# Low weight parts of three blocks by accumulating transfers, wider state products in two units, and a last block pair split by token halves

## The chip, the cores and the metric

The kernel runs on one core of one Trainium2 chip. The metric is the device time of one execution in microseconds. Of the kernel before, three runs took 699.57, 699.68 and 700.46 us; the median is 699.68 us. The profile is of one further execution.

## The reference

There are two steps. The first is a gated linear recurrence over 768 tokens, for 4 batches and 8 heads of 48 dimensions: a complex state of 48x48 per head is turned and damped by a complex factor per token and dimension, the product of key and value is added, and the query reads the real part.

```
mag = sqrt(a_re*a_re + a_im*a_im);  scale = minimum(mag, 0.999) / (mag + 1e-6)
for t in range(768):
    S_re, S_im = ar*S_re - ai*S_im + k[t] (x) v[t],  ar*S_im + ai*S_re
    y[t] = einsum('bhd,bhde->bhe', q[t], S_re)
```

The second is a feed-forward without a nonlinearity other than a product: `x = y` as 3072 tokens by 384, `out = ((x @ w_a) * (x @ w_b)) @ w_out`, with 1536 columns in the middle. All inputs and outputs are float32.

## The kernel before, in words

**Units.** The work is cut into 12 units: two pairs of batches by six chunks of 128 tokens. A unit holds 256 tokens (two batches, i = 0 and 1). Per unit there are four stages. *Preparation* (`prep`, VectorE with ScalarE's help): cumulated products of the complex factors within the chunk, by which queries and keys are multiplied (L308, L323) so that the recurrence becomes a masked product of queries and keys. *Stacking* (`stack`, L345): ten copies within on-chip memory, issued by SP, which lay the prepared queries and keys out by head. *Attention* (`attn`): scores (L378, then the mask on VectorE, L381), transposes of the keys (L389, L393), outputs (L418, cast at L422), the residual of the rounding (L428; in units 0 and 1 by a product with a negative identity, L430 and L433), and the state update (`state`, products at L441, added by VectorE at L448 or, in the first chunk, copied by ScalarE at L450). *Feed-forward*: twelve blocks f of 128 middle columns.

**Feed-forward in rounded parts.** TensorE multiplies in the rounded format float32r. So each operand is split into a high part, which is the value rounded, and a low part, the rest: x is xh+xl, the weights are hi+lo, h is hh+hl, and a product is made of three, high by high, high by low and low by high. `gemm1` makes the 18 products of a block (L485), ScalarE copies one half of the result (L493), VectorE multiplies by the other (L494), ScalarE rounds it (L495) and VectorE takes the rest (L496). `gemm2` multiplies by w_out: for each half of the tokens (tt) three products (L503) are added in an accumulator that runs over all twelve blocks. A list `pend` holds a block's hh and hl back, so that `gemm2` of a block follows two blocks behind `gemm1` (LAG = 2). Behind the last block of a unit `second` copies each half from its accumulator (L642) and stores it from ScalarE's queue (L643).

**Weights.** They arrive as 64-bit floats, seen as pairs of 32-bit words. `split_weights` makes, for each block f and each of its three parts m (w_a, w_b, w_out, 384 columns each), a float32 value t in a buffer named o_sb by three bit steps on VectorE (L133, L135, L137). ScalarE rounds t into hi (L141). TensorE forms t - hi in an accumulator by two products with the identity and the negative identity (L146, L147; the first is float32 and runs in two passes), and ScalarE rounds that into lo (L148). The buffer o_sb exists three times (O_BUFS = 3) and is also used for the output. Accumulators of the conversion come from the pool of `gemm1` for blocks 0 to 6 and from the attention's pool `pm`, which has two buffers, from block 7 on.

**Order.** Python generators interleave the stages. Six blocks are converted before the attention of unit 0; block 6+f is converted ahead of block f of unit 0's feed-forward (w = 0). In the same loop the preparation of unit 1 is drained: 3000 ns of its written-in costs per block, and the rest when f is 4 (P1_AT), where the stacking of unit 1 is emitted too; the pieces of unit 1's attention are handed out from f = 5 on. The framework then places the instructions on each engine's queue by priority: `tc.high_priority` lifts the steps of the attention and, by more, those of the feed-forward. Each engine executes its queue in order. In the trace unit 1's attention begins only behind nearly all of unit 0's feed-forward.

**The end.** Behind the last loop the pieces of `chk` are tested (up to L698), then `second` runs for the two blocks left in `pend` (L699, L700), and a branch on the test result would start a slow exact path (`token_by_token`), which is not taken with these inputs.

## Time and profile before

| | |
|---|---|
| three runs | 699.57, 699.68, 700.46 us |
| the profiled execution | 700.52 us, its span 698.8 us |
| TensorE, products / weight loads | 654.6 us (94%) / 610.4 us (87%) |
| VectorE | 550.4 us (79%) |
| ScalarE | 311.4 us (45%) |
| GpSimd | 5.6 us (1%), 11 instructions |
| chain that ended last | PE 64%, DVE 26%, DMA 4%, ACT 3% |
| mean granted TensorE clock | 0.972 |

The span is the time from the first to the last recorded event of the program; the rest of the execution's time lies around it. In the profile PE is TensorE (PEld its weight loads), DVE VectorE, ACT ScalarE, POOL GpSimd; SPq and ACTq are the issue of transfers by SP and ScalarE. L141 is line 141 of the kernel. In a timeline a row has the start in us, the duration in us (the sum where several instructions are merged, with their count behind x), the engine, the line, the operation, output<-inputs, and in brackets how long the engine had been idle and what released it. In the table of groups the two numbers after the bar are the busy time in us and the mean of one in ns. Matmuls are pipelined, so the duration of one is longer than the distance to the next.

### The profile page before, as it was taken

To read this page: it belongs to the slowest core of one execution; us is meant where nothing else is said; L and a number is where in the kernel's file an instruction comes from. 1 tells how busy PE (TensorE), PEld (TensorE's weight loads), DVE (VectorE), ACT (ScalarE), POOL (GpSimd) and SP (SyncE) were. 2 spreads that over 40 slices of the span, in tenths; PEclk is the share of its full clock that TensorE was granted. 3 is DMA by queue.
4 is the path that set the end of the run, shared out by engine and by line. 5 is a ranking of instruction groups with operands and counts; after the bars stand their busy time and mean duration, and the time that the engine had idled before them with its cause. 6 is when DMAs were issued, how large, how long until landed. Compare 5 with 4: busy or idle time off the path is not lost.

```text
span 698.8 us, 14287 instructions
## 1 busy us (share of the span) xinstructions
PE 654.6 (94%) x5842; PEld 610.4 (87%) x5842; DVE 550.4 (79%) x1259; ACT 311.4 (45%) x622; POOL 5.6 (1%) x11
## 2 busy tenths in 40 slices
PE   3547999999999999999999999999999999999996
PEld 1224788799899999999999999999999999999996
DVE  6998899998888989989899798999989863233221
ACT  6357656634535446255363564534542332231221
POOL 3000000000000000000000000000000000000000
PEclk9567999999999999999999999999999999999999
DMA  8963300611414205124151340511510500300000
GB/s 312 403 262 93 120 1 0 180 58 58 130 38 130 81 21 157 58 88 132 32 161 45 93 143 2 166 69 47 135 55 2 162 27 17 106 23 2 24 1 27
DMA packets 30231, 63.93 MB, mean 91 GB/s; under 512 B 3664, under 2 KB 7248, under 8 KB 30160
## 3 DMA queue, kind: packets, MB, share of 16 engines
q1 hardware_dynamic: 26704, 58.23, 26.6%
q10 hardware_dynamic: 3456, 4.72, 1.9%
q8 instruction: 48, 0.79, 0.4%
q14 instruction: 23, 0.19, 0.1%
HBM read 39.32 MB, written 4.72 MB: 63 GB/s over the span
## 4 chain that ended last, share of the span: by engine, by line
PE 64%; DVE 26%; DMA 4%; ACT 3%; issue 2%; SPq 1%; DVEq 0%; ACTq 0%
PE ab L485 31%; PE o L503 15%; PE xp L418 6%; PE pm L378 4%; PE pm L441 4%; DVE a_t L288 2%; DMA w<-in_dram 2%; DVE pr L226 2%; DVE qk L308 2%; DVE h_t L494 2%; PE pm L389 2%; DVE hl L496 2%; DMA stk<-qk 1%; DVE am L381 1%; DVE z L232 1%
## 5 line engine op out<-in xcount | busy, mean ns | idle before, releaser
L485 PE MATMUL ab<-xh,w 128*128 128x256 f32 x1728 | 338.7, 285 | 0.0
L485 PEld LDWEIGHTS ab<-xh,w 128*128 128x128 f32 x1728 | 276.6, 189 | 1.9 <-issue 1.4
L485 PE MATMUL ab<-xl,w 128*128 128x256 f32 x864 | 244.6, 283 | 0.0
L485 PEld LDWEIGHTS ab<-xl,w 128*128 128x128 f32 x864 | 162.9, 189 | 0.5 <-ACT xl L433 0.2
L503 PE MATMUL o<-w,hh 128*128 128x384 f32 x576 | 152.4, 345 | 0.0
L493 ACT COPY h_t<-ab 128x256 f32<-128x256 f32 x144 | 53.3, 370 | 184.5 <-PE ab L485 184.1
L494 DVE TENSOR_TENSOR h_t<-ab,h_t 128x256 f32<-128x256 f32 x144 | 60.6, 421 | 70.5 <-ACT h_t L493 69.8
L503 PEld LDWEIGHTS o<-w,hh 128*128 128x128 f32 x576 | 96.8, 188 | 3.7 <-issue 2.8
L503 PE MATMUL o<-w,hl 128*128 128x384 f32 x288 | 97.6, 340 | 0.0
L495 ACT CAST hh<-h_t 128x256 fp32r<-128x256 f32 x144 | 58.0, 403 | 72.6 <-DVE h_t L494 71.4
L496 DVE TENSOR_TENSOR hl<-h_t,hh 128x256 fp32r<-128x256 f32 x144 | 60.6, 421 | 15.6 <-ACT hh L495 15.5
L378 PE MATMUL pm<-stk 128*128 128x128 f32 x384 | 55.3, 282 | 2.6 <-DMA stk<-qk 1.8
L146 PE MATMUL ab<-o_sb,ident 128*128 128x384 f32 x42 | 29.3, 797 | 29.9 <-DVE o_sb L137 29.9
L378 PEld LDWEIGHTS pm<-stk 128*128 128x128 f32 x384 | 49.6, 193 | 7.6 <-issue 4.2
L503 PEld LDWEIGHTS o<-w,hl 128*128 128x128 f32 x288 | 54.0, 188 | 0.1
L226 DVE TENSOR_TENSOR pr<-z 128x384 f32<-128x384 f32 (+1 forms) x91 | 47.2, 525 | 4.3 <-ACT z L212 2.5
L288 DVE TENSOR_TENSOR a_t<-z,b_t 128x768 f32<-128x768 f32 x48 | 45.1, 953 | 0.0
L146 PEld LDWEIGHTS ab<-o_sb,ident 128*128 128x128 f32 x42 | 10.2, 288 | 39.5 <-DVE o_sb L137 29.2
L418 PE MATMUL xp<-am,v_t 128*32 128x128 f32 x768 | 42.5, 277 | 2.1 <-DVE am L381 1.8
L308 DVE TENSOR_TENSOR qk<-qk,z 128x1536 f32<-128x1536 f32 (+1 forms) x26 | 42.3, 1628 | 0.1
L381 DVE TENSOR_TENSOR am<-pm,mask 128x512 f32<-128x512 f32 x48 | 32.8, 686 | 6.7 <-PE pm L378 6.6
L441 PEld LDWEIGHTS pm<-v_t,kt 128*96 128x96 f32 x320 | 32.2, 164 | 1.8 <-issue 1.4
(106 smaller groups left out, 758.7 us busy)
## 6 DMA issues: line engine op xcount, KB each, us to landing
w<-in_dram SPq DMA_DIRECT2D x36, 384.0 KB, 8.1
qk<-in_dram SPq DMA_DIRECT2D x12, 768.0 KB, 4.8
stk<-qk SPq DMA_DIRECT2D x48, 192.0 KB, 3.4
a_t<-in_dram SPq DMA_DIRECT2D x11, 768.0 KB, 4.4
v_t<-in_dram SPq DMA_DIRECT2D x24, 256.0 KB, 2.7
stk<-qk SPq DMA_DIRECT2D x24, 192.8 KB, 3.4
out_dram<-o_sb ACTq DMA_DIRECT2D x24, 192.0 KB, 1.9
stk<-qk SPq DMA_DIRECT2D x16, 128.0 KB, 3.1
```

Source lines behind the costliest of these rows:

```text
L226: vec.tensor_tensor(out=pr[:, :, :, o:o + n], in0=view(zz, W + at_(i) + 2 * o, [[W, 2], [-W, 2], [2, n]]), in1=tok(slice(1, 3), i - 1, o, ...
L288: vec.tensor_tensor(out=pz[:, s].rearrange("p (j b e) -> p j b e", j=SUB // 2, e=2), in0=zb[:, 1 + s], in1=view(bb, (1 + k - s) * NB, [[0, ...
L308: vec.tensor_tensor(out=qk4[:, :, k, x0:x1], in0=qk4[:, :, 1, x0:x1], in1=z[:, k].rearrange("p (j t) -> p j t", j=NJ).unsqueeze(2).broadca ...
L378: pe.matmul(out=sp[:, h4], lhsT=stk[:, h, ks], rhs=stk[:, h, qs], start=True, stop=True)
L418: pe.matmul(out=xp[qd * 32:(qd + 1) * 32, ti], lhsT=l, rhs=rr, start=st, stop=sp_, tile_position=(0, qd * 32), skip_group_check=True)
L441: pe.matmul(out=kp[0:KS, h4 * D:(h4 + 1) * D], lhsT=kts[i, hg][:, h4, :], rhs=v_t[:, o:o + D], start=True, stop=True)
L485: pe.matmul(out=ab[:, m * TOK:(m + 1) * TOK], lhsT=r(w_ab(f, part, m * NJ + i)), rhs=r(xt[:, i, :]), start=n == 0, stop=n == 8)
L493: act.copy(out=h_t, in_=ab[:, 0:TOK])
L494: vec.tensor_tensor(out=h_t, in0=ab[:, TOK:2 * TOK], in1=h_t, op=ALU.mult)
L495: act.copy(out=r(hh), in_=h_t)
L496: vec.tensor_tensor(out=r(hl), in0=h_t, in1=hh, op=ALU.subtract)
L503: pe.matmul(out=os_[tt][:, 0:DM], lhsT=r(ht[:, ts]), rhs=r(w_t[f, 2][:, part, :]), start=(f == 0 and n == 0), stop=(f == NF - 1 and n == 2))
```

## The change

There are three edits.

**Low parts of blocks 9 to 11.** All weight parts are now kept negative: hi is the negated rounding of t. For blocks 0 to 8 TensorE forms t + hi with the identity (a rounded copy `rident` is made at the start), and lo is the negated result. For blocks 9 to 11 (DMA_FROM) a transfer issued by GpSimd adds hi onto t in its o_sb buffer, and ScalarE rounds the negated t into lo (`round_late`) after the next piece's transfer has been emitted; what is left is rounded one step after block 11. Two negated factors cancel in the product of w_a and w_b; the sign of w_out is undone where the output is copied.

```
-act.copy(out=r(hi), in_=t)
+act.mul(out=r(hi), in_=t, mul=-1.0)
+if f >= DMA_FROM:
+    nc.gpsimd.dma_start(out=t, in_=hi, accum_op=ALU.add)
+    late.append((lo, t))
+    if len(late) > 1:
+        round_late()
+    continue
...
-pe.matmul(out=lp[:, 0:n], lhsT=r(nident), rhs=r(hi), start=False, stop=True)
-act.copy(out=r(lo), in_=lp[:, 0:n])
+pe.matmul(out=lp[:, 0:n], lhsT=r(rident), rhs=r(hi), start=False, stop=True)
+act.mul(out=r(lo), in_=lp[:, 0:n], mul=-1.0)
...
+while late:
+    round_late()
+yield
```

**State products of units 0 and 1.** The product of a head's keys and values takes 96 columns of the value tile instead of the head's own 48 (n is 2*D there, D in the other units); the columns of the head are picked where the result is read.

```
+own = u >= OWN_FROM
+n = D if own else 2 * D
-o = (h // 2) * 128 + (h % 2) * 80
+o = (h // 2) * 128 + (h % 2) * (80 if own else 32)
-kv = view(kp[0:KS], 0, [[2 * D, 2], [D, 2], [1, D]])
+kv = view(kp[0:KS], 0, [[2 * n, 2], [D if own else 3 * D, 2], [1, D]])
```

**The last two blocks.** The six products of the first token half (blocks 10 and 11) come before the six of the second. The first half is copied by ScalarE and stored by SP; the second is copied half by ScalarE and half by VectorE, and stored in two transfers, from ScalarE's and from SP's queue.

```
-while pend:
-    second()
+for tt in range(2):
+    for w2, f2, hh, hl, os2 in pend:
+        gemm2(f2, hh, hl, os2, (tt,))
+    o_sb = moe.tile([128, DM], F32, name="o_sb", bufs=O_BUFS)
+    if tt == 0:
+        act.mul(out=o_sb, in_=os2[tt][:, 0:DM], mul=-1.0)
+        sync.dma_start(out=out_d[w2, tt], in_=o_sb)
+    else:
+        act.mul(out=o_sb[:, 0:DM // 2], in_=os2[tt][:, 0:DM // 2], mul=-1.0)
+        vec.tensor_scalar(out=o_sb[:, DM // 2:], in0=os2[tt][:, DM // 2:DM], scalar1=-1.0, scalar2=None, op0=ALU.mult)
+        act.dma_start(out=out_d[w2, tt, :, 0:DM // 2], in_=o_sb[:, 0:DM // 2])
+        sync.dma_start(out=out_d[w2, tt, :, DM // 2:], in_=o_sb[:, DM // 2:])
```

More of the change, by code (lines that the diff above doesn't have):

```diff
@@ L45 @@
 HB = 3
+OWN_FROM = 2
 O_BUFS = 3
 CONV_ON_AB = 7
+DMA_FROM = 9
 NCHK = NU * G + NU + 1
@@ L114, in tile_kernel @@
     act.mul(out=nident.bitcast(F32R), in_=ident, mul=-1.0)
+    rident = const.tile([128, 128], F32, name="rident")
+    act.copy(out=rident.bitcast(F32R), in_=ident)
     w_t = {}
@@ L125, in load_weights, with round_late @@
                            in_=w_d[f, :, c0:c0 + n].bitcast(U32))
+    late = []
+    def round_late():
+        lo, t = late.pop(0)
+        act.mul(out=r(lo), in_=t, mul=-1.0)
     def split_weights():
@@ L497, in gemm1, with gemm2 @@
         return hh, hl
-    def gemm2(f, hh, hl, os_):
-        for tt in range(2):
+    def gemm2(f, hh, hl, os_, tts=range(2)):
+        for tt in tts:
             ts = slice(tt * 128, (tt + 1) * 128)
@@ L597, in feed_forward @@
                     o_sb = p1.tile([128, DM], F32, name="o_sb")
-                    act.copy(out=o_sb, in_=os_[tt][:, 0:DM])
+                    act.mul(out=o_sb, in_=os_[tt][:, 0:DM], mul=-1.0)
                     sync.dma_start(out=out_v[bass.ds(c, 1), bp, tt].rearrange("o p m -> p (o m)"), in_=o_sb)
@@ L641, in second @@
                 with tc.high_priority(offset=MOE_FIRST):
-                    act.copy(out=o_sb, in_=os2[tt][:, 0:DM])
+                    act.mul(out=o_sb, in_=os2[tt][:, 0:DM], mul=-1.0)
                 act.dma_start(out=out_d[w2, tt], in_=o_sb)
@@ L698, in tile_kernel @@
     vec.tensor_scalar(out=bad, in0=tot[0:1, 0:1], scalar1=128.0 * NCHK, scalar2=None, op0=ALU.not_equal)
-    while pend:
-        second()
+    for tt in range(2):
[3 more added lines that the diff above has]
+        if tt == 0:
+            act.mul(out=o_sb, in_=os2[tt][:, 0:DM], mul=-1.0)
+            sync.dma_start(out=out_d[w2, tt], in_=o_sb)
[4 more added lines that the diff above has]
+            sync.dma_start(out=out_d[w2, tt, :, DM // 2:], in_=o_sb[:, DM // 2:])
     fast.close()
```

4 lines of the change are left out of this document (2 added, 2 removed).

## The prediction

> **What bounds the kernel now.** I read the busy times by stage first, then the chain of work that ended last, then the timelines around the three places that the change touches. The stages:
>
> ```profile
> core 0: us, PE busy (x) PEld busy (x) DVE busy (x) ACT busy (x) POOL busy (x), PEclk, DMA share, GB/s
> 78.00:90.00 12.00, 12.00 (x93) 10.84 (x93) 10.32 (x24) 10.88 (x23) 0.00 (x0) 1.00 0.16 46
> 90.00:128.00 38.00, 37.66 (x239) 33.17 (x238) 37.44 (x95) 20.48 (x47) 0.00 (x0) 1.00 0.07 22
> 128.00:150.00 22.00, 20.08 (x245) 17.24 (x245) 19.83 (x47) 12.77 (x22) 0.00 (x0) 1.00 0.48 139
> 180.00:500.00 320.00, 318.57 (x3092) 306.78 (x3091) 290.77 (x648) 154.19 (x295) 0.00 (x0) 1.00 0.29 87
> ```
>
> From 180 us TensorE is full (318.57 of 320) at full clock, and the change touches nothing there but the last two microseconds. So the end is set by the moment at which the feed-forward of unit 1 can begin (150 us in this trace), and by the tail. The stage in which the change works, 90 to 128 us, is full on two engines at once: TensorE 37.66 of 38, VectorE 37.44 of 38; ScalarE has 17.5 us free. The chain of work tells which of the two carries on into the next stage:
>
> ```profile
> 118.19 0.54 DVE o_sb L133 x2
> 118.72 0.47 DVE o_sb L135
> 119.53 0.47 DVE o_sb L137
> 119.99 0.87 DVE a_t L317
> 120.86 0.47 DVE o_sb L135
> 121.72 0.40 issue
> 122.12 0.55 DVE o_sb L137
> 122.67 0.87 DVE qk L323
> 123.87 1.67 DVE qk L308
> 125.87 1.11 DVE qk L308
> 126.98 0.48 issue
> 127.57 3.38 DMA stk<-qk
> ...
> 132.22 1.41 PE o L503 x8
> ```
>
> It is VectorE: the preparation of unit 1 (L317, L323, L308) ends at 127.5 us, the stacking copies leave at 127.57, and only with their landing can unit 1's attention begin. TensorE, though busy, is at that time finishing unit 0's products (L503), for which nothing waits but its own next work. In the chain the reader should see the weight conversion (o_sb) standing between steps of the preparation: 0.54+0.47+0.47 us before L317 and 0.47+0.55 us behind it.
>
> **Low parts of blocks 9 to 11: what leaves TensorE.** Nine pieces (three blocks by three parts) lose an identity product in two float32 passes and a rounded one:
>
> ```profile
> 82.95 0.65 PE pm L146 x2
> ```
>
> 0.65 us for the two passes, and for the third 1.41/8 = 0.18 us, as L503 has it in the chain above: 9 x 0.83 = 7.4 us of TensorE between 97 and 123 us, and two psum buffers less in demand. Counted as time at the end this is nothing by itself, because VectorE's steps are all kept: the three bit steps of a piece stay, and the two casts on ScalarE stay (the second now reads memory instead of psum; both forms are casts of 128x384):
>
> ```profile
> L141 ACT CAST w<-o_sb 128x384 fp32r<-128x384 f32 x36 | 18.1, 510 | 12.3 <-DVE o_sb L137 11.5 <-DMA w<-in_dram 0.6
> ```
>
> The sign of all weights costs nothing, a scaled copy in place of a copy; the extra rounded identity is one ScalarE step at the very start, before any weight has landed.
>
> **What is added.** Nine transfers within on-chip memory, each 192 KB, issued by GpSimd, whose queue the page shows empty after its first microseconds. The trace has no transfer of GpSimd and none that accumulates. The nearest are the stacking copies, on-chip to on-chip:
>
> ```profile
> stk<-qk SPq DMA_DIRECT2D x48, 192.0 KB, 3.4
> DMA to landing us min/median/max: 2.4/3.3/5.3
> ```
>
> I bound the landing by 2.4 and 5.3 us and take 3.4, the row of equal size; an accumulation can hardly land before a plain copy of the same size. No bandwidth is fought over: the DMA share in 90 to 128 us is 0.07. What the transfer changes is how long a piece keeps its o_sb buffer, of which there are three. Before, a buffer comes free when the identity product and the first cast have read it; now it must also wait for the landing and the rounding. The first five of the nine pieces run from here
>
> ```profile
> 97.06 0.35 DVE L133 TENSOR_SCALAR o_sb<-w 128x384 uint32<-128x384 uint32 x1
> ...
> 106.09 0.55 DVE L137 SCALAR_TENSOR_TENSOR o_sb<-w,o_sb 128x384 uint32<-128x384 uint32 x1
> ```
>
> to here: 9.6 us for five, 1.9 us apart, 5.7 us for one turn of three buffers. A turn now needs some 2.5 us of bit steps as they are interleaved, two casts of 0.51 us and 3.4 us: 6.9 us. So each of these pieces comes about (6.9-5.7)/3 = 0.4 us later, 2 us over the five, and VectorE takes steps of the preparation in the meantime, which stand beside them in its order. The whole nine take 25.6 us (97.06 to 122.67), 8.5 us a turn, so that the later ones are not held. Two microseconds later means that the last piece's two steps (0.47 and 0.55 us at 120.86 and 122.12) fall behind L323 and L308 and leave the path. This is the gain that I count: 1.0 us, between nothing (they stay where they are) and 2.5 us (all the conversion steps of the quoted chain leave it). The last rounding then comes near 130 us; unit 0's last products wait for it, and nothing waits for them before the attention of unit 1 is through.
>
> **What that stage gains behind 128 us.** The ten stacking copies are issued one behind the other:
>
> ```profile
> 127.57 7.06 SPq L345 DMA_DIRECT2D stk<-qk  x10
> ...
> 138.84 0.49 PE L378 MATMUL pm<-stk 128*128 128x128 f32 x2 [0.57 <-ACT kt L393]
> ```
>
> 0.71 us each, so the tenth lands at 127.57 + 9x0.71 + 3.4 = 137.3 us; the scores that use it start at 138.84, 1.5 us later, held by work that queues on TensorE (L503, 1.41 us in the chain) and by ScalarE. With 7.4 us taken off TensorE the products of blocks 9 and 10 are mostly done before 131 us. I take 0.8 us, between 0 and 1.5. Against that, VectorE's four steps for blocks 10 and 11 may come ahead of L308 rather than behind it; I count that at nothing, since they then leave the stretch behind, and take it into the upper bound.
>
> **96 columns.** Units 0 and 1 do their state products 96 wide:
>
> ```profile
> 144.21 0.64 PE pm L441 x8
> ...
> 145.63 0.81 PE pm L389 x8
> ```
>
> 48 columns take 80 ns an instruction, the transposes, which move 96 columns, 101 ns. So 21 ns more, 0.17 us for a group of eight. In unit 1 three of the four groups lie before the feed-forward can begin: +0.5 us. In unit 0 the cost lies beside full VectorE. Bounds: 0 (if loading the weights sets the 80 ns) and twice the 0.64 us, +1.9 us for the three. VectorE and ScalarE read the same 192 columns as before. The Trainium skill, "TensorE: Matmul & The Clock Gate", section "LDWEIGHTS (loading the stationary operand)", gives a load as its columns over 1.2 in ns, 80 ns for the 96 here, which is what the row has; by that rule the weight load sets the pace and the sum has 0 instead of 0.5 us.
>
> **The tail.**
>
> ```profile
> 691.16 0.42 DVE L496 TENSOR_TENSOR hl<-h_t,hh 128x256 fp32r<-128x256 f32 x1
> ...
> 692.92 0.34 PE L503 MATMUL o<-w,hl 128*128 128x384 f32 x1
> 693.27 0.34 ACTq L643 DMA_DIRECT2D out_dram<-o_sb  x1
> 693.70 0.48 ACT L642 COPY o_sb<-o 128x384 f32<-128x384 f32 x1 [0.47 <-PE o L503]
> 694.21 0.56 ACTq L643 DMA_DIRECT2D out_dram<-o_sb  x1
> L450 ACT COPY u<-pm 96x192 f32<-96x192 f32 x8 | 2.5, 314 | 1.4 <-PE pm L441 1.4
> ```
>
> The twelve last products are the same, in another order; block 11's low part is ready at 691.58 us, and the sixth product, the first to use it, would start near 691.7, so TensorE still ends at 693.26. Then, before, ScalarE is in the issue of the first store and begins the second copy at 693.70; the store leaves at 694.21. After, the first half's copy and store (now on SP) lie half a microsecond earlier, both engines begin at 693.28 with 192 columns each, 0.31 us by L450, and two stores leave near 693.62: 0.6 us earlier. The bytes are the same; what comes behind the landing follows unchanged. I take -0.6 us, between -0.3 (two stores each pay for themselves) and -0.7.
>
> **Sum.** -1.0 -0.8 +0.5 -0.6 = -1.9 us. The profiled execution took 700.52 us (span 698.8 and 1.7 around it), 0.84 us above the median of the runs, 699.68; taken off the median, 697.8 us. A measurement of this kernel tells apart about 0.2%, 1.4 us. What is late next: the preparation of unit 2, which takes over VectorE at 127.8 and gets the slipped steps; if its stacking comes later, TensorE has feed-forward of unit 1 to do.
>
> **Rivals.** *The transfer hides and frees nothing*: the order of VectorE stays as it is, the scores wait for ScalarE and not for TensorE. Then -0.6 and 0 to +0.5 remain: 699.3 us. For it: VectorE's 37.44 of 38 us, to which the change gives nothing back.
>
> *More conversion slips*: all 2.5 us of the chain, with 1.5 us behind it, and 0.5 and -0.6 as above: -4.1, 695.6 us. Against it: the ScalarE steps between L302 and L317 leave VectorE gaps that the conversion fills for nothing.
>
> *ScalarE stands before a landing*: its queue is in order, and the rounding of a piece waits for its transfer. Behind it are queued L303 and L304, on which L317 waits, and the h_t copies, on which VectorE waits. Where the landing comes later than the place that the rounding was given, everything behind is late by the difference. Four pieces fall between 114 and 123 us; at 5.3 instead of 3.4 us, 1.9 us each, 7.6 us; ScalarE's free time (17.5 of 38 us, 46%) hides that share of it, leaving +4.1 us on the stacking. With +0.5 and -0.6, 703.7 us; at half that lateness 701.6. It decides from about 0.75 us of lateness a piece (4x0.75x0.54 = 1.6 us).
>
> *VectorE stands before a buffer*: 8.5 us a turn less 2.5 and 1.0 leaves 5.0 us for issue and landing together. Beyond that VectorE itself waits, a third of the excess for each of nine pieces: at 6 us, 9x1.0/3 = +3.0 us; with the other terms 702.6 us. The Trainium skill, "SBUF — State Buffer", section "Who interferes with whom", says that descriptors of GpSimd's transfers are written through ports that VectorE's two-port instructions lock, and advises against hiding such a transfer under VectorE; no run here shows one, and VectorE is what is full here.
>
> **Chances.** Forecast 0.33 (own range 696.6 to 698.3), hidden 0.32, more slips 0.13, ScalarE before a landing 0.13, VectorE before a buffer 0.09. Faster by over 0.2%: 0.46; within: 0.32; slower: 0.22. The range: from 695.0, past the rival of more gain and its weaker tail, to 702.3, which takes half of the two slow ones.
>
> **What would show it.** Right: no L146 after 97 us; stacking of unit 1 near 126.5 us; an L137 of block 11 behind L308; the score that was at 138.84 within 1 us of the tenth landing; L441 groups of 0.8 us; last stores near 0.6 us after TensorE's end less than now. Wrong: ScalarE idle before the rounding with a DMA as releaser, or VectorE idle before L133 with ScalarE's rounding as releaser; stacking after 128 us; landings over 5 us. If the stacking is earlier and the feed-forward of unit 1 is not, the loss lies in TensorE's order between.

## The result: 8.7 us slower, and the profile after

| | before | after |
|---|---|---|
| median of the runs | 699.7 us | 708.36 us (707.54 to 709.52, 4 runs) |
| ratio, 95% interval | | 1.0121 [1.0108, 1.0133] |
| profiled execution, span | 700.52, 698.8 us | 707.54, 705.3 us |
| mean granted TensorE clock | 0.972 | 0.958 |
| unit 1: first stacking copy issued | 127.57 us | 126.04 us |
| unit 1: first product of the feed-forward | 149.38 us | 151.87 us |
| unit 2: first stacking copy issued | 172.39 us | 177.61 us |
| TensorE's last product ends | 693.26 us | 698.56 us |
| from there to the span's end | 5.5 us | 6.8 us |

A second measurement of the changed kernel (last experiment below) gave 1.0112 [1.0096, 1.0129]. Of the 7.0 us between the two profiled executions 5.3 are there when TensorE ends, 1.2 more come behind it, and 0.5 lie outside the span. The 1.2 us do not repeat in full: in the second trace of the changed kernel (e18) 6.0 us lie behind TensorE's end, and in seven traces below that have the tail of before it is 5.4 to 6.3 us.

First the stages of the kernel after, in the same windows as before (columns: length, busy time and count of each engine, TensorE's granted clock, share and rate of the transfers):

```profile
90.00:128.00 38.00, 33.82 (x233) 31.57 (x231) 35.11 (x87) 18.71 (x43) 4.73 (x6) 0.99 0.24 52
128.00:150.00 22.00, 19.10 (x217) 16.19 (x216) 17.65 (x36) 14.05 (x24) 3.10 (x4) 0.78 0.63 150
180.00:500.00 320.00, 317.63 (x3045) 304.66 (x3046) 286.76 (x634) 150.46 (x290) 0.00 (x0) 1.00 0.30 88
```

From 180 us on TensorE is almost as full as before (317.63 against 318.57 us). Between 90 and 150 us TensorE now idles 7.1 of 60 us (2.3 before), and in the second stretch its clock is 0.78 instead of 1.00, which takes another 0.22 x 19.1 = 4.2 us of work. That is 9.0 us lost, 1.6 more than the 7.4 us of identity products that went. Some of the 5.3 us lies earlier: the stacking of unit 0 is issued at 60.37 us (58.74 before), the clock of 50 to 70 and of 70 to 90 us is 0.60 and 0.91 (0.68 and 1.00), and busy time times clock up to 90 us is 43.3 us instead of 45.6. The signs alone (e4) do the same there and lose no time, since TensorE then fills 128 to 140 us (11.95 of 12 us, 10.33 before); in the whole change it waits in that stretch instead. The 1.6 and the 2.3 us make 3.9 of the 5.3; the rest is not assigned. A finer cut of the later stretch finds the place, before first, then after:

```profile
114.00:128.00 14.00, 13.90 (x92) 12.49 (x91) 13.87 (x25) 8.74 (x18) 0.00 (x0) 1.00 0.17 59
128.00:140.00 12.00, 10.33 (x95) 8.62 (x98) 11.06 (x23) 9.22 (x15) 0.00 (x0) 1.00 0.70 201
```

```profile
114.00:128.00 14.00, 9.82 (x62) 8.69 (x60) 13.31 (x25) 7.09 (x16) 2.03 (x3) 0.98 0.40 97
128.00:140.00 12.00, 9.22 (x56) 7.13 (x55) 8.80 (x17) 7.25 (x12) 3.10 (x4) 0.60 0.86 183
```

What it waited for stands in the chain of the kernel after (start, duration, what; steps of 0.04 us and less are left out):

```profile
118.55 0.83 POOL o_sb L153
119.38 8.27 issue
127.67 4.91 DMA o_sb<-w
132.60 0.53 ACT w L135
133.18 1.65 PE o L524 x4
134.83 0.85 PE pm L397 x4
135.72 0.80 PE pm L397 x2
```

Read it upwards. The scores of unit 1 (L397, L378 before) begin in earnest at 134.83 us. Ahead of them in TensorE's order stand four products of unit 0 (L524, L503 before), which wait for a low part; ScalarE rounds it (L135, `round_late`) only when the transfer has landed, 4.91 us after its issue at 127.67. This is the sixth of the nine pieces, block 10's part of w_out. The 8.27 us before its issue are a wait too: GpSimd waits for the cast L151, and that for the piece's last bit step, L147, which has slipped behind the preparation of unit 1 (L327, L308 before) to 126.27 us. The timeline has the idle time before each step:

```profile
126.27 0.55 DVE L147 SCALAR_TENSOR_TENSOR o_sb<-w,o_sb 128x384 uint32<-128x384 uint32 x1
126.85 0.53 ACT L151 ACTIVATE w<-o_sb 128x384 fp32r<-128x384 f32 x1 [2.06 <-DVE o_sb L147]
127.67 0.86 POOL L153 DMA_DIRECT2D o_sb<-w  x1 [8.29 <-ACT w L151]
...
132.60 0.52 ACT L135 ACTIVATE w<-o_sb 128x384 fp32r<-128x384 f32 x1 [2.81 <-DMA o_sb<-w]
133.18 0.69 PE L524 MATMUL o<-w,hh 128*128 128x384 f32 x1 [1.66 <-ACT w L135]
134.62 1.90 PE L397 MATMUL pm<-stk 128*128 128x128 f32 x6
```

Five rows of the table of waits of the kernel after, 90 to 160 us (who <- for whom: us, times, longest):

```profile
ACT w L135 <- DMA o_sb<-w: 8.2, 5, 2.8
DVE o_sb L143 <- ACT w L135: 3.2, 2, 2.2
PE ab L506 <- ACT w L135: 2.2, 2, 2.0
PE o L524 <- ACT w L151: 1.9, 1, 1.9
PE o L524 <- ACT w L135: 1.7, 1, 1.7
```

ScalarE stands before landings, VectorE before a buffer that a rounding frees, and TensorE before casts (L151, L141 before) and roundings that are late. The landing itself is 3.0 us in the median of the four transfers that run alone (98 to 118 us; the longest took 4.4). Of the five from 118 to 142 us, whose median is 4.9, the first and the last land in 3.2 and 3.0 us; the three issued while the stacking copies run, from 127.67 us on, take 4.9, 5.6 and 6.3. The stacking copies get slower too: their ten issues take 9.91 us (7.06 before), and those of 192.8 KB land in 3.7 us (3.2 before).

```profile
o_sb<-w POOLq DMA_DIRECT2D x4, 192.0 KB, 3.0
```

```profile
stk<-qk SPq DMA_DIRECT2D x6, 192.8 KB, 3.7
o_sb<-w POOLq DMA_DIRECT2D x5, 192.0 KB, 4.9
```

```profile
126.04 9.91 SPq L364 DMA_DIRECT2D stk<-qk  x10
```

The tail of the kernel after:

```profile
698.22 0.34 PE L524 MATMUL o<-w,hl 128*128 128x384 f32 x1
698.60 0.33 ACT L729 ACTIVATE o_sb<-o 128x192 f32<-128x192 f32 x1 [0.21 <-PE o L524]
698.96 0.34 ACTq L731 DMA_DIRECT2D out_dram<-o_sb  x1
698.96 0.36 DVE L730 TENSOR_SCALAR o_sb<-o 128x192 f32<-128x192 f32 x1 [2.06 <-ACT o_sb L729]
699.35 0.86 SPq L732 DMA_DIRECT2D out_dram<-o_sb  x1
```

VectorE's half copy begins when ScalarE's has ended, not beside it, and the span ends 5.1 us after the end of the last store's issue (705.3 - 700.21); in the kernel before it is 4.0 us (698.8 - 694.77).

### The profile page after: what moved, and what is told of

The parts are those of the page before. It is cut to its first block, busy times and chain, and to the rows that moved or that the text cites. A ratio compares the mean times of both kernels' runs of the same rounds, so it can differ in the third digit from the quotient of the medians.

```text
span 705.3 us, 14260 instructions
## 1 busy us (share of the span) xinstructions
PE 655.8 (93%) x5815; PEld 609.9 (86%) x5815; DVE 552.7 (78%) x1260; ACT 312.0 (44%) x623; POOL 13.4 (2%) x20
## 4 chain that ended last, share of the span: by engine, by line
PE 56%; DVE 30%; issue 5%; ACT 4%; DMA 3%; POOL 0%; SPq 0%; DVEq 0%; POOLq 0%; ACTq 0%
PE ab L506 26%; PE o L524 13%; PE xp L437 6%; PE pm L397 5%; PE pm L462 4%; DVE a_t L307 3%; DVE qk L327 3%; DVE pr L245 2%; DVE hl L517 2%; DVE h_t L515 2%; PE pm L408 2%; DVE z L312 2%; DVE z L251 1%; DMA stk<-qk 1%; DVE pb L280 1%
## 5 line engine op out<-in xcount | busy, mean ns | idle before, releaser
L524 PE MATMUL o<-w,hh 128*128 128x384 f32 x576 | 152.6, 346 | 3.7 <-ACT w L151 1.9
L524 PEld LDWEIGHTS o<-w,hh 128*128 128x128 f32 x576 | 97.1, 189 | 7.8 <-issue 3.0
L524 PE MATMUL o<-w,hl 128*128 128x384 f32 x288 | 97.8, 340 | 0.1
L397 PE MATMUL pm<-stk 128*128 128x128 f32 x384 | 59.1, 290 | 2.9 <-DMA stk<-qk 2.7
L397 PEld LDWEIGHTS pm<-stk 128*128 128x128 f32 x384 | 51.4, 198 | 9.2 <-issue 6.0
L524 PEld LDWEIGHTS o<-w,hl 128*128 128x128 f32 x288 | 54.4, 189 | 0.4 <-DVE hl L517 0.4
L437 PE MATMUL xp<-am,v_t 128*32 128x128 f32 x768 | 44.0, 281 | 2.9 <-DVE am L400 2.7
L327 DVE TENSOR_TENSOR qk<-qk,z 128x1536 f32<-128x1536 f32 (+1 forms) x26 | 42.4, 1629 | 0.1
L437 PE MATMUL xp<-stk,u 128*32 128x128 f32 x640 | 35.3, 274 | 0.0
## 6 DMA issues: line engine op xcount, KB each, us to landing
stk<-qk SPq DMA_DIRECT2D x48, 192.0 KB, 3.3
stk<-qk SPq DMA_DIRECT2D x24, 192.8 KB, 3.4
out_dram<-o_sb ACTq DMA_DIRECT2D x22, 192.0 KB, 1.9
```

Source lines behind the costliest of these rows:

```text
L327: vec.tensor_tensor(out=qk4[:, :, k, x0:x1], in0=qk4[:, :, 1, x0:x1], in1=z[:, k].rearrange("p (j t) -> p j t", j=NJ).unsqueeze(2).broadca ...
L397: pe.matmul(out=sp[:, h4], lhsT=stk[:, h, ks], rhs=stk[:, h, qs], start=True, stop=True)
L437: pe.matmul(out=xp[qd * 32:(qd + 1) * 32, ti], lhsT=l, rhs=rr, start=st, stop=sp_, tile_position=(0, qd * 32), skip_group_check=True)
L524: pe.matmul(out=os_[tt][:, 0:DM], lhsT=r(ht[:, ts]), rhs=r(w_t[f, 2][:, part, :]), start=(f == 0 and n == 0), stop=(f == NF - 1 and n == 2))
```

## The experiments

The first theory was that the landing of the transfers carries the loss; the rivals were the tail, the wider products and the signs, and then the ways in which a landing can act. Each letter (theory A, B, C, D) holds for the run whose expectation names it; A for ScalarE's queue, B for the buffers, C for the missing work and D for TensorE's queue run through the transfers' part. A ratio is to the kernel before on the same chip; 0.1% is 0.7 us.

| kernel | edit | median us | ratio [95%] |
|---|---|---|---|
| e1_tail | tail alone | 701.13 | 1.0012 [1.0001, 1.0024] |
| e2_cols | 96 columns alone | 698.07 | 0.9962 [0.9946, 0.9978] |
| e3_dma | signs and transfers | 705.76 | 1.0071 [1.0054, 1.0088] |
| e4_sign | signs alone | 700.52 | 1.0002 [0.9990, 1.0014] |
| e5_dma_cols | e3 and 96 columns | 706.75 | 1.0082 [1.0067, 1.0096] |
| e7_dma_pool | e3, GpSimd rounds | 710.31 | 1.0152 [1.0137, 1.0166] |
| e9_no_transfer | e3 without the transfers | 700.80 | 1.0010 [0.9999, 1.0022] |
| e8_cols_tail | e2, tail on ScalarE's queue | 698.86 | 0.9981 [0.9972, 0.9991] |
| e10_own_memory | e3, o_sb free at once | 704.22 | 1.0066 [1.0051, 1.0080] |
| e11_own_memory_deep | e10, rounding three back | 704.79 | 1.0065 [1.0053, 1.0077] |
| e12_early_blocks | e3 for blocks 6 to 8 | 715.71 | 1.0225 [1.0202, 1.0249] |
| e13_halves | e2, token halves | 697.88 | 0.9970 [0.9958, 0.9982] |
| e14_no_round | e10 without rounding | 702.16 | 1.0030 [1.0016, 1.0044] |
| e15_no_transfer_cols | e9 and 96 columns | 698.69 | 0.9979 [0.9964, 0.9993] |
| e16_conv5 | before, five blocks ahead | 700.96 | 1.0010 [1.0000, 1.0019] |
| e17_best | e13 and e16 | 699.75 | 1.0001 [0.9989, 1.0014] |
| e18_after_again | the whole change | 707.88 | 1.0112 [1.0096, 1.0129] |
| e19_after_halves | the change, tail of e13 | 707.89 | 1.0102 [1.0082, 1.0122] |

### The four parts alone

**The tail.** The loop of the diff over token halves in place of `second`, with plain copies.

> Only the last two blocks by token halves, weights unsigned, everything else as before. In the profile of the change the span's end lies 6.8 us behind TensorE's last product against 5.5 us before, VectorE's half copy begins only when ScalarE's has ended, and SP's last store is issued at 0.8 us behind that product. Theory 1 (the tail itself lost what it was to save): slower than before by 1.0 to 1.6 us. Theory 2 (the tail saves 0.6 us as predicted and the late end came from elsewhere): faster by 0.3 to 0.7 us.

**The 96 columns.** OWN_FROM = 2 and the four lines of `state`.

> Only the 96 columns in units 0 and 1. Theory 1 (the weight load or the 96 columns set the pace, no change of order): 0 to +0.7 us. Theory 2 (the wider products also change the order in which the engines work and carry a part of the 8.7 us): slower by 2 us or more, with the stacking of unit 1 later than 127.6 us or the feed-forward of unit 1 later than 150 us.

**The transfers** with the signs that they need.

```
+OWN_FROM = 0
 DMA_FROM = 9
```

> Only the low parts of blocks 9 to 11 by accumulating transfers, with the sign of all weights; 48 columns and the old end. Theory 1 (ScalarE stands before landings and VectorE before buffers; this part carries the loss): slower by 5 to 8 us, ScalarE idle for 6 us or more with a transfer onto o_sb as releaser, the feed-forward of unit 1 at 151 us or later. Theory 2 (the three parts lose together through the order of work, none alone): within 2 us of before.

**The signs.**

```
+DMA_FROM = NF
```

> Only the sign of all weights (scaled copies, the rounded positive identity), every low part by products on TensorE, 48 columns, the old end. Theory 1 (the sign costs nothing): within 0.7 us of before. Theory 2 (scaled copies or the extra identity at the start delay unit 0, whose stacking came 1.6 us later in the change): slower by 1.5 us or more, stacking of unit 0 at 60 us or later.

The signs cost nothing that can be measured, the tail 0.8 us (0.1 to 1.7 by its interval), the transfers 5.0, and the columns do not cost but gain 2.7 us, which neither theory had. The transfers alone leave TensorE's end at 698.38 us, where the whole change has 698.56: the columns' gain is missing in the whole. Where the columns gain shows in their windows:

```profile
114.00:128.00 14.00, 14.00 (x95) 12.86 (x94) 13.84 (x24) 7.49 (x17) 0.00 (x0) 1.00 0.39 111
128.00:140.00 12.00, 12.00 (x137) 10.50 (x135) 10.82 (x24) 9.01 (x15) 0.00 (x0) 1.00 0.47 138
```

TensorE has no gap: 26.00 us busy, 24.23 before. The stacking of unit 1 is issued at 123.23 us instead of 127.57, and unit 0's last products (the last row starts at 150.17 us, 133.84 before) lie between the steps of unit 1's attention and fill the waits there.

### Does the columns' gain add to the transfers?

```
-OWN_FROM = 0
+OWN_FROM = 2
 DMA_FROM = 9
```

> The changed kernel with the tail of before: negated weights, accumulating transfers and 96 columns. Alone, the transfers cost 5.0 us (TensorE's last product at 698.38 us of the trace) and the columns gained 2.7. Theory A, the landings set x: once ScalarE and VectorE stand before transfers between 114 and 136 us, the feed-forward of unit 1 begins when they let it, and the order that the columns change no longer matters; then this kernel is as slow as the transfers alone or a little slower, +5 to +7.5 us against before, and the tail adds only its own 0.8 to 1.5 us to the 8.7 of the whole change. Theory B, the two parts add: +2.3 us, about 702; then about 6 us of the whole change come from the tail, which the trace of the changed kernel does not show.

1.0082 against 1.0071 for the transfers alone: no gain of 2.7 us is left, theory A. Without a landing it is there (0.9979 against 1.0010):

```
-nc.gpsimd.dma_start(out=t, in_=hi, accum_op=ALU.add)
+OWN_FROM = 2
```

> The kernel without transfers (the nine low parts are rounded from the weights themselves, nothing is subtracted) with the 96 columns added; tail of before. Without transfers and with 48 columns it was 700.8, its trace 1.7 us better at TensorE's end than before. If it is the landing alone that takes the columns' gain away, the gain is here: 1 to 3 us below the 48-column one, 697.5 to 700. If the two exclude each other in any case, because both come from the same slip of block 11's steps behind L308, it is within 1 us of the 48-column one, 700 to 701.5.

So the landing takes it away, and the two do not exclude each other.

### Is it the landing, or the missing work?

```
-nc.gpsimd.dma_start(out=t, in_=hi, accum_op=ALU.add)
```

> The transfers alone, less the transfers: the nine low parts are rounded from the weights themselves, nothing is subtracted (this part of the computation is left out), so neither an issue nor a landing is waited for; the identity products stay out of TensorE. Theory A or B, the landing (by ScalarE's queue or by the buffers) carries the loss: this kernel is as fast as before or faster, 696 to 700. Theory C, it is not the landing but that TensorE lacks the 7.4 us of identity products that kept it busy while VectorE prepared unit 1, so that its granted clock falls to 0.5 between 126 and 138 us: then the loss stays, 702 to 706, with the clock of that stretch below 0.8.

The loss is gone (1.0010, the interval holds 1), with the identity products still out of TensorE. Theory C falls as a cause of the loss, though its sign is there: the clock of 128 to 140 us is 0.89, and TensorE idles.

```profile
114.00:128.00 14.00, 11.24 (x65) 10.06 (x64) 14.00 (x24) 7.26 (x16) 0.00 (x0) 0.85 0.37 107
128.00:140.00 12.00, 10.41 (x116) 9.07 (x114) 9.19 (x20) 8.32 (x14) 0.00 (x0) 0.89 0.54 159
```

In this order of work that is the most that leaving the 7.4 us out could bring: TensorE idles 4.3 us of these 26 and runs slower, so even a transfer that lands at once gains nothing that could be measured; nor does it beside the columns (0.9979 with no landing, 0.9962 with the identity products in place).

### Who stands before the landing?

**GpSimd rounds** in place of ScalarE:

```
-act.mul(out=r(lo), in_=t, mul=-1.0)
+nc.gpsimd.tensor_scalar(out=r(lo), in0=t, scalar1=-1.0, scalar2=None, op0=ALU.mult)
```

> The transfers alone (negated weights, 48 columns, tail of before), with the rounding of a landed piece done by GpSimd, which has nothing else to do, in place of ScalarE. No ScalarE instruction then waits for a landing of a piece. Theory A, ScalarE's queue: its copies for the preparation and the score path no longer stand behind a landing, ScalarE's waits with a transfer of the pieces as releaser (11.1 us between 90 and 160) are gone, and most of the 5.0 us comes back: within 2 us of before, 698 to 702. Theory B, the buffers: VectorE's bit steps wait for a buffer that is held through issue, landing and rounding, whoever rounds; GpSimd's rounding is slower than ScalarE's, so VectorE's waits for a buffer grow and the loss stays or rises, 704 to 708.

Twice the loss. ScalarE no longer waits for landings, and it did not help, as theory B said. But B's reason carries little of it: VectorE's wait for a buffer is 1.7 us (0.2 in e3). TensorE waits 6.5 us for roundings (5.8 in e3), and ScalarE's copies of the transposed keys, in unit 1's attention, wait 9.0 us for TensorE (3.0 in e3):

```profile
ACT kt L412 <- PE pm L408: 9.0, 2, 7.8
PE ab L506 <- POOL w L135: 6.5, 2, 3.9
DVE o_sb L143 <- POOL w L135: 1.7, 1, 1.7
```

```profile
110.22 2.68 POOL L135 TENSOR_SCALAR w<-o_sb 128x384 fp32r<-128x384 f32 x1 [2.23 <-DMA o_sb<-w]
136.47 1.16 POOL L135 TENSOR_SCALAR w<-o_sb 128x384 fp32r<-128x384 f32 x1 [2.89 <-DMA o_sb<-w]
```

A rounding takes GpSimd 1.16 to 2.68 us (0.52 on ScalarE), and the low parts come later still. That gave theory D: what counts is when TensorE gets the low part, since its queue holds the readers ahead of unit 1's attention.

**The buffer.** The piece is copied to its place, the transfer adds there, and the rounding is done in place, one piece back and three pieces back:

```
-nc.gpsimd.dma_start(out=t, in_=hi, accum_op=ALU.add)
+act.copy(out=r(lo), in_=t)
+nc.gpsimd.dma_start(out=r(lo), in_=r(hi), accum_op=ALU.add)
-if len(late) > 1:          (e11: > 3)
```

> The transfers alone (48 columns, tail of before), but each piece is first copied by ScalarE into the place of its low part (nine more steps of 0.51 us), the transfer accumulates there, and the o_sb buffer is free once ScalarE has read it; the rounding still stands one piece behind in ScalarE's order. The copy rounds, so that the low parts of these blocks come out as zero: the subtraction is left out as arithmetic, not as work. The trace of the kernel without the transfers ended TensorE at 691.51 us, with them at 698.38. Theory B, the held buffers: VectorE's bit steps no longer wait for a landing and most of the loss goes, 699 to 702. Theory A or D, ScalarE's queue or TensorE's own queue before weights that come late: the landing is as late as before for both, 704 to 707.

> As the kernel with the transfer into the low part's own place, but the rounding stands three pieces behind instead of one, so that ScalarE meets it when its transfer has long landed. Low parts come out as zero here too. Theory A, ScalarE's queue: its waits with a transfer of the pieces as releaser fall below 1 us, and with the buffers free as well the time is near that of the kernel without transfers, 699 to 702, where the other of this pair stays at 704 or more. Theory D, TensorE's queue: unit 0's last products stand in TensorE's order before the scores of unit 1 and wait for the last low parts, which now come even later; the loss stays or grows, 704 to 708, with TensorE's waits for L135 as large as before (5.8 us between 90 and 160).

Neither moves the time beyond the intervals, so the buffers (B) do not carry the loss of e3, where VectorE waits 0.2 us for one. Both have nine copies more on ScalarE, which could hide a small gain. The 3.2 us of the whole change come with the columns (3.4 in e5) and were not tried by themselves. The three-back form does not do what it was made for: ScalarE still waits 8.7 us with a transfer as releaser, among them 2.5 us at 123.88 and 2.2 at 133.21, because the last pieces' bit steps come so late (126.7 to 129.7 us) that nothing is left to put between transfer and rounding. So it told A and D not apart.

**Nothing rounds behind the landing**; TensorE waits for it itself:

```
 nc.gpsimd.dma_start(out=r(lo), in_=r(hi), accum_op=ALU.add)
-late.append(lo)
-if len(late) > 1:
-    round_late()
```

> As the kernel with the transfer into the low part's own place (48 columns, tail of before), but nothing rounds behind the landing: the transfer's result is used as it lies, so no ScalarE step waits for a landing, and TensorE's products wait for it themselves. The nine roundings are left out as work. Theory A, ScalarE's queue before landings: the loss goes, 698 to 701. Theory D, the landing comes too late for TensorE, whose in-order queue holds the products of blocks 9 to 11 ahead of unit 1's scores: it stays, 703 to 706, and TensorE now waits with the transfers of the pieces as releaser for over 3 us between 110 and 140.

1.0030, between the two theories. Against 1.0066 with the rounding it is 0.36% or 2.5 us better, and the intervals do not meet: the nine roundings in ScalarE's queue, their waits with their work, carry about half of the loss. It is not the work of these steps: e3, with nine roundings where this kernel has nine copies, runs as many ScalarE steps and has 1.0071, and those intervals do not meet either. Against no transfer (1.0010) 1.4 us are left, with intervals that do meet, and these rows of the kernel without rounding say where:

```profile
PE ab L504 <- DMA w<-w: 2.2, 2, 1.9
PE pm L395 <- DMA stk<-qk: 1.5, 1, 1.5
```

TensorE waits for the landing of low parts (2.2 us, over 3 expected) and for stacking copies that share the transfers' time. So it is shown that a rounding which must wait for its landing costs about half of the loss. Whether it costs through ScalarE's later steps (A) or through low parts that reach TensorE later (D) is not separated: this kernel takes both away, and e7, which took only ScalarE's waits away, lost more.

**Earlier blocks.**

```
-if f >= DMA_FROM:
+if 6 <= f < 9:
```

> The transfers alone (48 columns, tail of before), but for blocks 6 to 8 instead of 9 to 11; the last three blocks keep the identity products. Everything is computed. Theory A and B, a landing holds ScalarE's queue and the buffers wherever it stands: VectorE is as full at 80 to 105 us as later, so the loss is of the same size, 703 to 707. Theory D, the place: the last blocks' low parts are what unit 0's last products wait for, directly ahead of unit 1's scores in TensorE's order; blocks 6 to 8 have other products to cover them, so the loss goes, 698 to 701, with TensorE's waits for L135 below 1 us.

Theory D named the last blocks as the bad place; the early ones are three times as bad, 715.71 us, and more than A and B expected too. There (60 to 105 us) the transfers meet the stacking copies of unit 0, for which TensorE waits with nothing else to do:

```profile
PE pm L398 <- DMA stk<-qk: 9.3, 4, 6.4
ACT w L136 <- DMA o_sb<-w: 9.2, 6, 1.8
```

```profile
o_sb<-w POOLq DMA_DIRECT2D x9, 192.0 KB, 4.9
stk<-qk SPq DMA_DIRECT2D x6, 192.0 KB, 4.8
```

Before, the six stacking copies of 192.0 KB in that stretch landed in 3.1 us. So there is a third path, which neither ScalarE's nor TensorE's queue explains: the two kinds of transfer are both slower when they run side by side, and the scores wait for one of them. The first six of the nine transfers, beside stacking copies and input loads, land in 4.8 to 5.8 us, the last three in 2.9 to 3.2. The changed kernel has this path too: in the trace of e18 the chain of work runs through the slowed stacking copies, the last of which lands at 138.09 us. What it costs there was not tried by itself.

### Why do the columns gain?

In their trace block 11's bit steps slip behind L308, the slip that the prediction had expected of the transfers. Five blocks ahead instead of six make that slip alone:

```
-CONV_FIRST = 6
+CONV_FIRST = 5
```

> The kernel before with one number changed: five blocks of weights instead of six are put into the order ahead of unit 0's attention, so that each later block, block 11 too, stands one block further back. Everything is computed. Theory A, the columns gained because the bit steps of block 11 slipped behind the preparation of unit 1: then this gains as much without any 96 columns, 696.5 to 698.5, with stacking of unit 1 at 122.5 to 125 in the trace (127.57 before). Theory B, the columns' gain has another source: within 0.2% of before, 698.5 to 701.3.

> 96 columns, token halves with whole copies stored by ScalarE, and five instead of six blocks ahead. Without the last it was 697.88. If the columns' gain is the slip of block 11, the slip is there already and a further one is late for TensorE's products of block 11: the same or a little slower, 697.5 to 700. If the two are separate, 695.5 to 697.

The stacking is 3.8 us earlier (123.75 us) and the time is not: 1.0010 [1.0000, 1.0019]. Theory A is not borne out. The windows of e16:

```profile
114.00:128.00 14.00, 13.54 (x90) 12.27 (x90) 13.95 (x26) 7.33 (x17) 0.00 (x0) 1.00 0.35 104
128.00:140.00 12.00, 11.03 (x113) 8.19 (x111) 11.41 (x23) 9.43 (x16) 0.00 (x0) 1.00 0.52 146
```

TensorE is busy 24.57 of 26 us (26.00 with the columns, 24.23 before): block 11 is converted so late that unit 0's last products wait with it, until 153.52 us. In this stretch an earlier stacking is worth only as much as TensorE has unit 0's products ready to put beside unit 1's attention. That the columns reach that mix is seen; why wider products move the order so is not settled. Added to the columns, the same number takes their gain away (1.0001).

But five blocks ahead is not the slip alone. It also leaves TensorE less to do before the scores of unit 0: in 50 to 70 us e16 is busy 14.75 us at a clock of 0.50, the kernel before 15.14 us at 0.68, some 2.9 us of work less. e17 has the same there (14.58 us at 0.50), while its 114 to 140 us are as full as with the columns alone (26.00 of 26 us). So in these traces the columns' gain goes in the early stretch, and what the slip alone is worth stays open.

### The tail

Three stores from ScalarE's queue, the half copies in two buffers (e8); whole halves by ScalarE (e13); the latter in the whole change (e19) beside the change itself (e18):

```
 if tt == 0: act.copy(o_sb); act.dma_start(o_sb)
 else:       act.copy(o_a, first half); vec.tensor_copy(o_b, second half)
             act.dma_start(o_a); act.dma_start(o_b)          (e8)
 for tt in range(2): gemm2(..., (tt,)); act.copy(o_sb); act.dma_start(o_sb)   (e13, e19)
```

> 96 columns alone, with a third form of the tail: token halves, the second half copied by ScalarE and VectorE into two separate buffers, and all three stores issued by ScalarE. Columns alone gave 698.07, 2.7 us under before. Theory A: the token-half tail lost 0.8 us because VectorE's half copy waited for ScalarE's (they write one buffer) and because the store on SP's queue put SP's branch at the end of the program behind it; then this one is 0.3 to 0.8 us faster than columns alone, 697.3 to 697.8, and the span ends under 5.5 us after TensorE. Theory B: it is the two last stores themselves that cost: then it is slower than columns alone by 0.3 to 0.8 us, 698.4 to 698.9.

> 96 columns alone, with the last two blocks by token halves, each half copied whole by ScalarE and stored from ScalarE's queue (no store from SP, no copy by VectorE). Columns alone: 698.07, TensorE's end to span's end 5.85 us in the trace. Theory A, the order by token halves is right and the split copies and SP's store were what cost: the first half's copy and store lie under TensorE's last six products, the second copy begins when they end, 0.4 us sooner; 0.3 to 0.5 us faster than columns alone, 697.6 to 697.8. Theory B, the order brings nothing, as what comes behind the last landing sets the end: within 0.2 us of columns alone.

> The changed kernel itself once more, as the measure for the run beside it. Transfers with columns gave +5.7 us, the tail alone +0.8. If the parts add, this is +6.5, 706 to 707.5 where before is 700; if the tail costs more inside the change, +8 to +9, 708 to 709.5.

> The changed kernel with the last token halves copied whole by ScalarE and stored from ScalarE's queue: no store from SP, no copy by VectorE; transfers and columns as in the change. With the columns alone this tail was as fast as the tail of before (0.9970 against 0.9962). Theory A, SP's store and the serialized half copies are all that the tail costs: 0.8 to 1.5 us under the run beside it, and the span ends under 6 us after TensorE's last product (6.8 in the changed kernel). Theory B, the difference lies between chips: then it is within 0.5 us of the run beside it.

The copies stay one behind the other in separate buffers (VectorE's row of e8, and the last store 0.98 us behind the one before it), so one buffer was not the reason; both read one accumulator.

```profile
691.14 0.88 ACTq L715 DMA_DIRECT2D out_dram<-o_sb  x1
691.14 0.36 DVE L714 COPY o_sb<-o 128x192 f32<-128x192 f32 x1 [2.29 <-ACT o_sb L713]
692.12 0.39 ACTq L716 DMA_DIRECT2D out_dram<-o_sb  x1
```

With whole halves the second copy still waits for the first store's issue, as in the kernel before:

```profile
690.41 0.34 ACTq L708 DMA_DIRECT2D out_dram<-o_sb  x1
690.85 0.48 ACT L707 COPY o_sb<-o 128x384 f32<-128x384 f32 x1 [0.47 <-PE o L506]
691.36 0.92 ACTq L708 DMA_DIRECT2D out_dram<-o_sb  x1
```

It is as fast as the columns with the old tail (0.9970 and 0.9962), not faster, as theory B of e13 had it. What SP's store costs is in the spans: from the end of the last store's issue to the span's end it is 5.0, 5.1 and 4.9 us where SP issues it (e1, the change, e18), and 4.0, 4.5, 4.0, 3.9 and 4.3 where ScalarE does (before, e2, e8, e13, e19). Some 0.9 us, about what the tail alone costs. This does not settle it: from the start of that issue the two groups overlap (5.2 to 6.0 and 4.4 to 5.3 us), and e8, without a store from SP, stands 0.19% above e2, near what its theory B (two last stores cost) had, though those intervals meet. Inside the change the two tails can't be told apart (1.0112 and 1.0102), e19 ends 6.1 us behind TensorE and not under 6, and e5 and e1 together give 0.94% where the whole gives 1.12 and 1.21%. The intervals of e5 and e1 added reach 1.20%, so the parts may add; up to 2 us more for the whole stay open.

## Why the prediction was wrong

Forecast 697.8 us, its range to 702.3; 708.36 came. The signs of both slow rivals, which were given 703.7 and 702.6, are in the trace.

- **What bounds the kernel: half right.** TensorE is full from 180 us on, and the stage before sets the end. But the forecast took the stacking of unit 1 as the time that carries over. It came 1.5 us earlier (126.04, forecast near 126.5), and the feed-forward of unit 1 2.5 us later. The forecast's own last line had named this case: the loss lies in TensorE's order between.
- **The step that failed** is the reading of TensorE at 127 us, "finishing unit 0's products (L503), for which nothing waits but its own next work". With it the wait of these products for a late low part was put at nothing. The forecast thought only of the last low part, and of that one it was right: one of block 11's products runs at 147.82 us and five from 156.24 on, behind nearly all of unit 1's attention. But the sixth part is late as well. At 133.18 us four products of block 10 stand in TensorE's queue ahead of the scores, behind 1.66 us of idle time, and the scores behind them (e18 has the same at 133.50). An engine's own order is a wait, also for work that needs nothing of what stands ahead. In all TensorE waits 5.8 us for casts and roundings between 90 and 160 us, and its clock falls. That the landings carry the transfers' loss is shown (1.0071 with, 1.0010 without); how it divides between TensorE's order, ScalarE's queue and the slowed stacking copies is read from waits and stays open. The last rounding was forecast near 130 us and began at 141.22.
- **Landing 3.4 us, no bandwidth fought over: wrong where it mattered.** 3.0 us in the median of the four alone, but 4.9, 5.6 and 6.3 for the three beside stacking copies, two of them above the upper bound of 5.3; landings over 5 us were also among the forecast's signs of being wrong. The forecast had looked at the share of 90 to 128 us (0.07), but the last transfers slip to 127 to 141 us, and the share of 128 to 150 us was 0.48 before, in a row that it had quoted.
- **Slips behind L323 and L308: right, but no gain is seen.** They did slip, and further than forecast: L147 of the last four pieces comes at 126.27 us and later, behind the second L327, which was L308. This took the transfers of these pieces to the time of the stacking copies. e16 has the slip without transfers and gains no time, but it loses work at 50 to 70 us as well, so whether the slip in itself is worth the 1.0 us is open.
- **0.8 us behind 128 us: wrong.** The scores were to be held less by TensorE, as its queue would be emptier. The queue was held instead.
- **7.4 us off TensorE counted as nothing: right**, and e9 bears it out: 1.0010 without landing.
- **96 columns, +0.5 us: wrong.** By themselves they gain 2.7 us, and in the change this gain is gone. A group of eight takes 0.85 us at 150.35 in the kernel after (0.81 forecast, 0.64 for 48 columns), so the price of an instruction was right; what the forecast left out is that the order of work changes. The Trainium skill, "TensorE: Matmul & The Clock Gate", section "LDWEIGHTS (loading the stationary operand)", would have 80 ns for each by the load; the row has 106.

```profile
150.35 0.85 PE pm L462 x8
```

- **The tail, -0.6 us: wrong, +0.8 alone.** The last store's issue starts 0.79 us after TensorE's end instead of 0.95, so 0.16 us of the 0.6 came: the half copies ran one behind the other. "What comes behind the landing follows unchanged" did not hold: from the end of the last issue to the span's end it is some 0.9 us more with SP's store. Which part of the tail costs the 0.8 us is open, as said.
- **Rivals.** ScalarE before a landing (8.2 us of waits, forecast 7.6 with 4.1 on the path) and VectorE before a buffer (3.2 us) are both in the table of waits. Of the first it is shown that roundings which wait cost time (e14); the second was not separated. The rule of the Trainium skill, "SBUF — State Buffer", section "Who interferes with whom", that VectorE's two-port instructions keep GpSimd from writing the descriptors of its transfers, does not account for the slow ones here, as far as the trace shows: the issues take 0.84 to 1.19 us, the transfer at 118.54 landed in 3.2 us with VectorE busy all the time, and the one at 127.67 in 4.9 us with VectorE busy 3.30 us of it. Which of VectorE's instructions were two-port ones the trace does not tell.

The first rival's +4.0 (703.7) is near the transfers' own +5.0, but by luck: it had the stacking of unit 1 4.1 us later, and it came 1.5 us earlier. It is far from the +8.7: it had -0.6 for the tail, which alone is +0.8, and up to 2 us stay open as said.

## What to carry to other kernels

A step taken off a full engine is worth nothing until one knows what that engine will do instead; here, as the waits show, it stood in its own order before the very results that had been moved to a slower path. Before a step goes to a transfer, follow its result to the reader, and look at what stands behind that reader in the same queue and which transfers run at the time to which the step will slip. And test parts alone: here the one part with a cost in the forecast was the one that gained, and 96 columns with the tail of before (0.9962 [0.9946, 0.9978], 2.7 us) are the fastest complete version found, though e13 (0.9970) can't be told from it.

## What the runs showed of the hardware

- In the kernel after, TensorE's granted clock is 0.60 over 128 to 140 us, where it has idled some 4 us in the 14 before; 9.22 us busy then do the work of 5.5. In e10 it is 0.62 behind 5.7 us of idle time, in the kernel before and in e16 1.00 behind less than 0.5 us. So its waits cost more than their length.
- An accumulating transfer of 192 KB within on-chip memory lands in 3.0 us alone (median of four in the kernel after) and in 4.9 to 6.3 beside stacking copies; these go from 3.1 to 4.8 us beside such transfers (e12).
- From the end of the last store's issue to the end of the span it is 4.9 to 5.1 us with SP (three traces) and 3.9 to 4.5 with ScalarE (five). The cause was not tried, and from the start of the issue the two overlap.
- A rounding of 128x384 takes GpSimd 1.16 to 2.68 us and ScalarE 0.52, so in e7 the step behind a landing took two to five times as long on the idle GpSimd.
- A ScalarE and a VectorE copy of two halves of one accumulator ran one behind the other in all three kernels that had them, also with separate buffers. Whether the accumulator or the order written by the framework does it was not tried.
